# Three pairs turned on TensorE instead of by DMA, ch2 weights in column halves, and another order of the output units

## The chip, the cores and the metric

The kernel runs on one core of one Trainium2 chip. The time is device time in microseconds (us) of one execution. The kernel before takes 389.54 us (median of 3 runs, 389.31 to 390.26); the profiled execution has a span of 388.6 us from the first to the last instruction.

## The reference

Cosine attention is followed by an MLP mixer. There are 8 batches, 12 heads, 448 positions and a head size of 64.

```python
q_n = q / (np.linalg.norm(q, axis=-1, keepdims=True) + 1e-06)
k_n = k / (np.linalg.norm(k, axis=-1, keepdims=True) + 1e-06)
scores = np.matmul(q_n, k_n.transpose(0, 1, 3, 2)) / tau
scores = scores - np.max(scores, axis=-1, keepdims=True)
attn = np.exp(scores)
attn = attn / (np.sum(attn, axis=-1, keepdims=True) + 1e-09)
x = np.matmul(attn, v)                       # then heads side by side: [8, 448, 768]
h = np.maximum(x^T @ w_tok1, 0.0) @ w_tok2   # over positions: 448 -> 256 -> 448
u = x + h^T
h2 = np.maximum(u @ w_ch1, 0.0) @ w_ch2      # over channels: 768 -> 1536 -> 768
out = u + h2
```

All inputs and the output are float32.

## The kernel before

**Pairs.** The work runs over 48 pairs of heads (six pairs for each batch, `NPAIR`; `i` is the pair's number). For a pair, q and k are loaded by DMA, squared (GpSimd, or ScalarE early on), summed over the head (VectorE, `sums`), turned into reciprocal norms (`norms`: ScalarE, then VectorE) and scaled into a float16 tile `kq` (`scaled`, GpSimd). This tile has to be turned, so that the head's channels lie on the partitions; the turned tile is `qk`. `score` (L323) multiplies k against q into PSUM tiles `psS`, and ScalarE takes the exponential into `pt` (L324). Each pair has three such score tiles ahead of the first unit and a fourth after it: of the same kind up to pair 11, and from pair 12 on a smaller one (`score_rest`, tile `psQ`, L330) for the 64 rows that 3 x 128 leave over. `pv_rest` (L345) and `pv` (L362) multiply `pt` with v into two tiles `psO`, and VectorE divides (L365, L366) into `x`. `tok1` (tile `psR`, L393, result `rt`, L396) and `tok2` (tile `psU`, L407, result `u`, L410) are the mixer over positions. The result `u` is turned by DMA into `ut` (`udma`, L416), or for a few early pairs on TensorE.

**Turning kq.** Pairs below `DMA_T0` = 13 are turned on TensorE by `tpose`: eight transposes into a PSUM tile `pst` (L300) and a copy on VectorE into `qk` (L302). Pairs from 13 on are turned by a DMA transpose that SyncE issues (`tpose_dma`, L308). `side` also decides by `DMA_T0` where the load of the pair six ahead stands in SyncE's queue: ahead of everything for the earlier pairs, behind the DMA transpose for the later ones.

**Units.** The mixer over channels is cut into units that are put into a list (`refill`), batch by batch: twelve units of `m_ch1` (tile `psG`, six matmuls, L433, emptied by ScalarE at L436), then the units of `m_ch2` (tile `psF`, twelve matmuls, L449). A ch2 unit computes one column half (384 of 768) of one tile of 128 output rows; VectorE adds `u` to it into an output tile `ost` (L453), and after the second half SyncE writes it out (L468, L474). 448 rows are three tiles of 128 rows and 64 rows more; the 64 rows of two neighbouring batches share one tile, m = 3, which is computed with the odd batch. Its sum takes two VectorE instructions of 64 rows each, because the two halves come from two batches.

**Order of the work.** It is written out by hand. The main loop over pairs issues: the three score tiles; `pv_rest` and `pv` of the pair before; `side` (loads and the norms and scaling of later pairs); a first unit; `psQ`; `tok2` of pair i-2; `tpose` of the next pair if it is turned on TensorE; further units as long as the due matmul time (`fed`) asks for them; `tok1` of pair i-1. Below, a segment is what lies between two groups of score tiles. A segment thus has a first unit, right behind `pv`, and none to several last ones between `tok2` and `tok1`.

**PSUM.** Two pools share the banks. `ps` has two narrow buffers of one bank each (tag "b"), taken in turn by `pst`, `psO`, `psR`, `psU` and by units called without `wide`. `ps2` has three buffers of two banks each (tag "s"), taken in turn by `psS`, `psQ` and by units called with `wide`. A new tile waits until the tile before it in the same buffer has been read.

**Weights.** `weights_ch2` loads `moe_w_ch2` with two DMAs from GpSimd, which also convert to float16. Each takes half of the 1536 rows and all 768 columns; they are issued in `side` at pairs 8 and 10. Each ch2 unit needs all 1536 rows of its column half.

**The end.** After the last pair's scores there are a unit (`unit()`, narrow), the last `pv`, a few wide units, the last `tok1` and `tok2`, and then all units of the last batch.

Of the kernel before, what the change touches and what calls it, by code (L numbers as in the profile page):

```python
# [7 lines left out]
FP32 = mybir.dt.float32  # L8
# [14 lines left out]
def kernel(  # L23
# [12 lines left out]
    nc = tc.nc  # L36

    B, H, S, E = q.shape
    D = H * E
# [7 lines left out]
    DH = 384  # L47
# [3 lines left out]
    NHALF = 2 * B  # L51
    inv_tau = 1.0 / float(tau)
    EPS_NORM = 1e-6
    DMA_T0 = 13
    OLD = 2 * NPAIR


# [15 lines left out]
    def pieces(lo, hi):  # L73
        got = []
        while lo < hi:
            c = lo // SC
            end = min(hi, SC * (c + 1))
            got.append((c, lo - SC * c, end - SC * c))
            lo = end
        return got  # L80
# [6 lines left out]
    outp = ctx.enter_context(tc.tile_pool(name="outp", bufs=3))  # L87
# [33 lines left out]
    def load_qk(i):  # L121
        b, h0 = i // NPAIR, 2 * (i % NPAIR)
        n = i // HP
        half.setdefault(n, {})
        st = pipe[i] = {}
        st["q"] = qkv.tile([SC, QS, E], FP32, name=f"qf_{i}", tag="qf")
        nc.sync.dma_start(out=st["q"][:].rearrange("p (g c) e -> p g (c e)", g=2),
                          in_=q[b, h0:h0 + 2].rearrange("g (p c) e -> p g (c e)", c=NCH))
        st["k"] = load_rows(i, "k", k[b], 7)
        if not old(i) and "kr" not in half[n]:  # L130
            half[n]["kr"] = load_rest(i, "k", k[b])

    def load_v(i):
        pipe[i]["v"] = load_rows(i, "v", v[i // NPAIR], 4)
        if not old(i) and "vr" not in half[i // HP]:
            half[i // HP]["vr"] = load_rest(i, "v", v[i // NPAIR])
# [13 lines left out]
    wc2t = cst.tile([128, CT, D], FP16, name="wc2t")  # L150
# [40 lines left out]
                            in_=moe_w_ch1[128 * t:128 * t + 384, cols].rearrange("(t p) c -> p t c", p=128))  # L191

    def weights_ch2(i):
        nc.gpsimd.dma_start(out=wc2t[:, 6 * i:6 * i + 6, :],
                            in_=moe_w_ch2[768 * i:768 * (i + 1)].rearrange("(t p) d -> p t d", p=128))

# [11 lines left out]
    def cast_v(i):  # L210
        vt = vts[(i // HP) % NV]
        if old(i):
            nc.gpsimd.tensor_copy(out=vt[0:SC, i % HP, :, 0:E], in_=pipe[i]["v"][:])
            return
        nc.gpsimd.tensor_copy(out=vt[:, i % HP, 0:2 * KC, 0:E], in_=pipe[i]["v"][:])
        if i % HP == 0:
            nc.gpsimd.tensor_copy(out=vt[:, :, 2 * KC, 0:E], in_=half[i // HP]["vr"][:])
# [21 lines left out]
    def squares(i):  # L239
        square(i, 0)  # L240
        square(i, 1)
# [13 lines left out]
    def norms(i, a0=0, a1=2, dve=False):  # L255
        st = pipe[i]
        n, sl = some(i, a0, a1)
        rn = st["rn"][0:n, sl]
        ne = nes[i % 3][0:n, sl]
        if dve:  # L260
            nc.vector.tensor_reduce(out=rn, in_=ne, axis=AXX.X, op=ALU.add)
            nc.vector.reciprocal(out=rn, in_=rn)  # L262
            return
        nc.scalar.activation(out=rn, in_=st["ssq"][0:n, sl], func=AF.Ln, bias=tiny[0:n])
        nc.scalar.activation(out=ne[:, :, 0], in_=rn, func=AF.Exp, scale=0.5)
# [21 lines left out]
    def scaled(i):  # L287
        scale(i, 0)
        scale(i, 1)
# [14 lines left out]
    def tpose_dma(i):  # L304
        st = pipe[i]
        qk = att.tile([128, 2 * NCH * 128], FP16, name=f"qk_{i}", tag="qk")
        st["qk"] = qk[:].rearrange("p (a c s) -> p a c s", a=2, c=NCH)
        nc.sync.dma_start_transpose(out=st["qk"].rearrange("p a c s -> p (a c) s"),  # L308
                                    in_=st["kq16"][:].rearrange("p a c g e -> p (a c g e)"))
# [88 lines left out]
    def tok2(i, pe=False, wide=False):  # L398
        st = pipe[i]
        b, pj = i // NPAIR, i % NPAIR  # L400
        if pj == 0:
            u16[b] = mix.tile([128, DT, 4, 128], FP16, name=f"u16_{b}", tag="u16", bufs=4)
            ut[b] = mix.tile([128, DT, 4, 128], FP16, name=f"ut_{b}", tag="ut")
        psU = (ps2 if wide else ps).tile([128, 4, 128], FP32, name=f"psU_{i}", tag="s" if wide else "b")
        for m, lo in enumerate(windows(b)):
            for tt in range(TT):
                nc.tensor.matmul(psU[:, m], w2t[:, tt, lo:lo + 128], st["rt"][:, tt],  # L407
                                 start=(tt == 0), stop=(tt == TT - 1))
        u = u16[b][:, pj]
        nc.vector.tensor_tensor(out=u, in0=psU[:], in1=st["x"][:], op=ALU.add)  # L410
        if not pe:
            udma(i)
# [25 lines left out]
    ost = {}  # L438


    def m_ch2(b, m, lo, hi, st, wide):
        gt = gts[b // 2]
        at = 384 if m == 3 else 128 * m + (b % 2) * 512
        if lo == 0:
            ost[0] = outp.tile([128, D], FP32, name=f"ost_{b}_{m}", tag="ost")
        o = ost[0]
        psF = (ps2 if wide else ps).tile([128, 512], FP32, name=f"psF_{b}_{m}_{lo}", tag="s" if wide else "b")
        for ct in range(CT):
            nc.tensor.matmul(psF[:, 0:hi - lo], gt[:, ct, at:at + 128], wc2t[:, ct, lo:hi],  # L449
                             start=(ct == 0), stop=(ct == CT - 1))  # L450

        def add(p0, p1, bb, slot):
            nc.vector.tensor_tensor(out=o[p0:p1, lo:hi].rearrange("p (j e) -> p j e", e=128),  # L453
                                    in0=psF[p0:p1, 0:hi - lo].rearrange("p (j e) -> p j e", e=128),
                                    in1=u16[bb][p0:p1, lo // 128:hi // 128, slot], op=ALU.add)

        if m < 3:
            add(0, 128, b, m + b % 2)
        else:
            add(0, 64, b - 1, 3)  # L460
            add(64, 128, b, 0)
        if st is None:
            return
        if m < 3:
            r = 0
            for n, (c, p0, p1) in enumerate(pieces(*MAIN[m])):
                eng = nc.scalar if st and n == 0 else nc.sync
                eng.dma_start(out=out[b].rearrange("(p c) d -> c p d", c=NCH)[c, p0:p1, st:hi],  # L468
                              in_=o[r:r + p1 - p0, st:hi])
                r += p1 - p0  # L470
        else:
            (c, p0, p1), = pieces(384, S)
            for bb, r in ((b - 1, 0), (b, 64)):
                nc.sync.dma_start(out=out[bb].rearrange("(p c) d -> c p d", c=NCH)[c, p0:p1], in_=o[r:r + 64])  # L474

    def ns(cols, n=1):
        return n * (cols / 2.4 + 2.5)
# [4 lines left out]
    def ch2_units(b):  # L482
        cuts = ((0, DH, None), (DH, D, 0))
        ends = ((0, DH, None), (DH, D - 128, 0), (D - 128, D, D - 128))
        return [(ns(hi - lo, CT), lambda wide, m=m, lo=lo, hi=hi, st=st: m_ch2(b, m, lo, hi, st, wide))
                for m in ((3, 0, 1, 2) if b == B - 1 else range(3 + b % 2))
                for lo, hi, st in (ends if (b, m) == (B - 1, 2) else cuts)]

    queue = []
    fed = [0.0, 0.0]  # L490
# [1 line left out]
    def unit(wide=False):  # L492
        if queue:
            t, fn = queue.pop(0)
            fn(wide)
            fed[0] -= t
# [6 lines left out]
    def refill(b):  # L503
        new = ch1_units(b) + ch2_units(b)
        fed[1] = (sum(t for t, _ in new) - (KEPT if b == 0 else 0.0)) / (NPAIR + 1 if b == 0 else NPAIR)
        queue.extend(new)

    with tc.manual_schedule():
        for i in range(3):
# [9 lines left out]
            name=nc.get_next_instruction_name(), act_func_set_id=ACT_SET_LN_EXP,  # L519
# [77 lines left out]
        i = NPAIR  # L597
# [22 lines left out]
        def side(i):  # L620
            if i + 6 < NP_ALL and i + 2 < DMA_T0:
                load_qk(i + 6)
            cast_v(i)
            if i + 3 < NP_ALL:
                squares(i + 3)
            if i in (8, 10):
                weights_ch2((i - 8) // 2)
            if i + 2 < NP_ALL:
                norms(i + 2)
                norms(i + 2, dve=True)  # L630
                scaled(i + 2)
                if i + 2 >= DMA_T0:
                    tpose_dma(i + 2)
            if i + 6 < NP_ALL and i + 2 >= DMA_T0:
                load_qk(i + 6)
            if i + 4 < NP_ALL:
                load_v(i + 4)

        for i in range(NPAIR + 1, NP_ALL):
            b, pj = i // NPAIR, i % NPAIR  # L640
# [12 lines left out]
            elif pj == 2 and b > 1:  # L653
                refill(b - 1)
            side(i)
            fed[0] += fed[1]
            unit(True)
# [4 lines left out]
            if i > NPAIR + 1:  # L662
                tok2(i - 2)
            if i + 1 < DMA_T0:
                tpose(i + 1)
# [5 lines left out]
            if i + 3 < NP_ALL:  # L671
                sums(i + 3)
        last = NP_ALL - 1
        unit()
        pv_rest(last)
        pv(last, 0)
        pv(last, 1)
# [45 lines left out]
```

## Time and profile before

| What | Value |
|---|---|
| Time, median of 3 runs | 389.54 us |
| Span of the profiled execution | 388.6 us |
| TensorE busy with matmuls | 371.9 us (96%) |
| GpSimd, ScalarE, VectorE busy | 237.4, 226.5, 216.7 us |
| psG, psF matmuls (L433, L449) | 116.6 and 116.2 us |
| Score tiles psS (L323) | 41.9 us in 312 matmuls |
| Transposes pst (L300) | 7.9 us in 104 matmuls |
| Copies qk<-pst (L302), 128x1024 | 0.68 us for one |
| DMA transposes qk<-kq (L308) | 35, median 3.1 us from issue to landing |
| wc2t loads (L194) | 2 of 1152 KB (float16), 12.1 and 13.6 us to landing |

The profile gives each instruction's start and length per engine, the idle time before it and who ended that idle time. Ends of matmuls are modelled, and neighbouring matmuls overlap in it, so their lengths add up to more than the time they take. The distance between the starts of two groups is the safer measure. A wait is named by the instruction that came last before it ended. The chain of work is followed back from the last instruction of the kernel.

### The profile page before, as it was taken

How to read it: one execution, taken by the hardware profiler on the slowest of the kernel's cores; microseconds unless marked ns; L12 is line 12 of the kernel's file. 1: busy time of each engine (PE TensorE's matmuls, PEld its weight loads, DVE VectorE, ACT ScalarE, POOL GpSimd, SP SyncE). 2: the span in 40 equal slices, each digit the busy share in tenths (PEclk: the TensorE clock that was granted, in tenths of full speed). 3: DMA queues.
4: the chain of work that ended last, by engine and by line, in shares of the span. 5: the costliest groups of instructions: out<-in, count | busy, mean ns of one | idle time of the engine just before them, and what ended most of it. 6: DMA issues, size and time to landing. Idle time of an engine off the chain costs nothing.

```text
span 388.6 us, 10171 instructions
## 1 busy us (share of the span) xinstructions
PE 371.9 (96%) x4100; PEld 241.4 (62%) x4100; DVE 216.7 (56%) x517; ACT 226.5 (58%) x398; POOL 237.4 (61%) x383
## 2 busy tenths in 40 slices
PE   5889999979999999999999999999999999999995
PEld 5566666656657666667657666667656666565563
DVE  7799766766437574557536674557545673241031
ACT  5999687745666447846665447855665456501500
POOL 8899979877667587577567577678567642000000
PEclk9899999999999999999999999999999999999999
DMA  8999999999976977869896999859974854013022
GB/s 223 273 224 234 178 251 214 196 191 192 235 180 143 205 178 192 200 152 176 209 182 130 222 181 199 165 145 189 224 179 117 164 123 96 14 56 96 0 75 89
DMA packets 117055, 65.00 MB, mean 167 GB/s; under 512 B 74896, under 2 KB 113424, under 8 KB 117008
## 3 DMA queue, kind: packets, MB, share of 16 engines
q1 hardware_dynamic: 112112, 58.41, 68.8%
q0 software_dynamic: 4080, 5.21, 7.9%
q10 hardware_dynamic: 816, 0.73, 0.7%
q8 instruction: 32, 0.52, 0.6%
q14 instruction: 15, 0.12, 0.1%
HBM read 43.45 MB, written 11.01 MB: 140 GB/s over the span
## 4 chain that ended last, share of the span: by engine, by line
PE 84%; ACT 7%; DVE 3%; DMA 2%; POOL 1%; issue 1%; ACTq 0%; DVEq 0%; POOLq 0%
PE psG L433 28%; PE psF L449 27%; PE psO L362 9%; PE psS L323 7%; PE psU L407 5%; ACT pt L324 5%; PE psR L393 4%; PE psQ L330 2%; PE psO L345 1%; ACT sq L235 1%; DMA qk<-kq 1%; DVE ost L453 1%; DMA qf<-in_q_dram 1%; DVE ssq L253 1%; PE pst L300 1%
## 5 line engine op out<-in xcount | busy, mean ns | idle before, releaser
L324 ACT ACTIVATE pt<-psS 128x896 f16<-128x896 f32 (+1 forms) x156 | 132.5, 916 | 58.5 <-PE psS L323 58.5
L433 PE MATMUL psG<-ut,wc1t 128*128 128x448 f16 x576 | 116.6, 352 | 0.2 <-ACT gt L436 0.2
L449 PE MATMUL psF<-wc2t,gt 128*128 128x384 f16 (+2 forms) x684 | 116.2, 323 | 0.0
L276 POOL TENSOR_TENSOR kq<-kf,rn 128x384 f16<-128x384 f32 (+1 forms) x48 | 42.8, 892 | 76.7 <-DVE rn L262 72.5
L436 ACT ACTIVATE gt<-psG 128x448 f16<-128x448 f32 x96 | 51.8, 540 | 63.4 <-PE psG L433 63.4
L449 PEld LDWEIGHTS <-gt 128*128 128x128 f16 x684 | 64.3, 98 | 38.0
L433 PEld LDWEIGHTS <-wc1t 128*128 128x128 f16 x576 | 53.9, 98 | 44.5 <-issue 0.3
L453 DVE TENSOR_TENSOR ost<-psF,u 128x384 f32<-128x384 f32 (+2 forms) x65 | 34.7, 534 | 60.6 <-PE psF L449 59.1
L253 DVE TENSOR_REDUCE ssq<-sq 128x15 f32<-128x960 f32 (+2 forms) x49 | 55.8, 1141 | 4.1 <-ACT sq L235 2.3
L396 DVE TENSOR_SCALAR rt<-psR 128x256 f16<-128x256 f32 x48 | 20.2, 420 | 59.5 <-PE psR L393 59.4
L276 POOL TENSOR_TENSOR kq<-qf,rn 112x512 f16<-112x512 f32 x45 | 46.9, 1043 | 3.0
L323 PE MATMUL psS<-qk 64*128 64x448 f16 x312 | 41.9, 357 | 6.4 <-DVE qk L302 2.5
L362 PE MATMUL psO<-vt,pt 128*128 128x65 f16 (+1 forms) x1056 | 40.3, 193 | 0.2 <-DVE ut L424 0.2
L237 POOL TENSOR_TENSOR sq<-qf 112x512 f32<-112x512 f32 x39 | 40.5, 1039 | 0.0
L237 POOL TENSOR_TENSOR sq<-kf 128x384 f32<-128x384 f32 (+1 forms) x46 | 40.1, 872 | 0.0
L362 PEld LDWEIGHTS <-pt 128*128 128x128 f16 (+1 forms) x1056 | 35.2, 97 | 4.0 <-PE psS L323 1.0
L366 DVE TENSOR_TENSOR x<-psO,rec 128x256 f16<-128x256 f32 x84 | 35.7, 425 | 2.9
L410 DVE TENSOR_TENSOR u<-psU,x 128x512 f16<-128x512 f32 x48 | 32.4, 674 | 4.8 <-PE psU L407 3.6
L393 PEld LDWEIGHTS <-w1t 128*128 128x128 f16 x384 | 24.9, 98 | 8.6 <-issue 1.9
L407 PEld LDWEIGHTS <-w2t 128*128 128x128 f16 x384 | 24.9, 98 | 7.8 <-issue 1.5
L407 PE MATMUL psU<-rt,w2t 128*128 128x128 f16 x384 | 29.3, 219 | 0.2 <-DVE qk L302 0.2
L393 PE MATMUL psR<-x,w1t 128*128 128x128 f16 x384 | 29.3, 219 | 0.0
(54 smaller groups left out, 277.3 us busy)
## 6 DMA issues: line engine op xcount, KB each, us to landing
qf<-in_q_dram SPq DMA_DIRECT2D x48, 224.0 KB, 3.6
kf<-in_k_dram SPq DMA_DIRECT2D x36, 192.0 KB, 3.5
vf<-in_v_dram SPq DMA_DIRECT2D x36, 192.0 KB, 3.9
vf<-in_v_dram SPq DMA_DIRECT2D x12, 224.0 KB, 7.2
out_dram<-ost SPq DMA_DIRECT2D x8, 336.0 KB, 3.3
wc1t<-in_moe_w_ch_dram POOLq DMA_DIRECT2D x4, 576.0 KB, 9.8
wc2t<-in_moe_w_ch_dram POOLq DMA_DIRECT2D x2, 1152.0 KB, 12.8
out_dram<-ost SPq DMA_DIRECT2D x8, 288.0 KB, 3.3
```

Source lines behind the costliest of these rows:

```text
L237: nc.gpsimd.tensor_mul(out=dst, in0=src, in1=src)
L253: nc.vector.tensor_reduce(out=st["ssq"][0:n, sl], in_=st["sq"][0:n, sl], axis=AXX.X, op=ALU.add)
L276: eng.tensor_tensor(out=kq[0:p, a, 0:n].rearrange("p c g e -> p g c e"), in0=st["kq"[a]][:].rearrange("p (g c) e -> p g c e", g=2), in1=_b ...
L323: nc.tensor.matmul(psS[:, hh, 0:S], qk[hb, c * n:c * n + 128], qm[hb], start=True, stop=True)
L324: nc.scalar.activation(out=pts[i % 2][0:n, 2 * S * c:2 * S * (c + 1)].rearrange("p (h s) -> p h s", h=2), in_=psS[0:n, :, 0:S], func=AF.Ex ...
L362: nc.tensor.matmul(psO[:, m, 0:E + 1], pts[i % 2][0:n, at:at + 128], vt[0:n, i % HP, nch * hh + c, 0:E + 1], start=(old(i) and c == 0), st ...
L393: nc.tensor.matmul(psR[:, tt], w1t[:, w1[m], tt * 128:(tt + 1) * 128], st["x"][:, m], start=(m == 0), stop=(m == 3))
L407: nc.tensor.matmul(psU[:, m], w2t[:, tt, lo:lo + 128], st["rt"][:, tt], start=(tt == 0), stop=(tt == TT - 1))
L433: nc.tensor.matmul(psG[:, 0:S], wc1t[:, dt, ct * 128:(ct + 1) * 128], ut[b][:, dt].rearrange("p m s -> p (m s)")[:, lo:lo + S], start=(dt ...
L436: nc.scalar.activation(out=gt[:, ct, (b % 2) * S:(b % 2 + 1) * S], in_=psG[:, 0:S], func=AF.Relu)
L449: nc.tensor.matmul(psF[:, 0:hi - lo], gt[:, ct, at:at + 128], wc2t[:, ct, lo:hi], start=(ct == 0), stop=(ct == CT - 1))
L453: nc.vector.tensor_tensor(out=o[p0:p1, lo:hi].rearrange("p (j e) -> p j e", e=128), in0=psF[p0:p1, 0:hi - lo].rearrange("p (j e) -> p j e" ...
```

## The change

Four things are changed, each with what it needs.

- Pairs 13, 14 and 15 are turned on TensorE like the pairs before them (`DMA_T0` = 16). The first pair whose scores wait for a DMA transpose is then pair 16. The loads in `side` move with it.
- The ch2 weights come in two column halves in place of row halves, the second one pair later (pair 11). Batch 0's units take the left half of all three row tiles first and the right half after, so that the second load has more time. Three output tiles are then open at once, hence `ost[m]` in place of `ost[0]`.
- In the other even batches nothing changes. In the odd batches 1, 3 and 5 the left half of the rest row tile (m = 3) is moved one place ahead in the list, so that it is the first unit of its segment and not the last. The last batch keeps its order.
- The unit after the last pair's scores takes a wide PSUM buffer, so that the two narrow ones are left to `psO`.

```diff
-    DMA_T0 = 13
+    DMA_T0 = 16
...
     def weights_ch2(i):
-        nc.gpsimd.dma_start(out=wc2t[:, 6 * i:6 * i + 6, :],
-                            in_=moe_w_ch2[768 * i:768 * (i + 1)].rearrange("(t p) d -> p t d", p=128))
+        cols = slice(DH * i, DH * (i + 1))
+        nc.gpsimd.dma_start(out=wc2t[:, :, cols], in_=moe_w_ch2[:, cols].rearrange("(t p) d -> p t d", p=128))
...
-            ost[0] = outp.tile([128, D], FP32, name=f"ost_{b}_{m}", tag="ost")
-        o = ost[0]
+            ost[m] = outp.tile([128, D], FP32, name=f"ost_{b}_{m}", tag="ost")
+        o = ost[m]
...
+        if b == B - 1:
+            order = [(m, c) for m in (3, 0, 1, 2) for c in (ends if m == 2 else cuts)]
+        elif b == 0:
+            order = [(m, c) for c in cuts for m in range(3)]
+        else:
+            order = [(m, c) for m in range(3) for c in cuts]
+            if b % 2:
+                order[5:5] = [(3, cuts[0])]
+                order.append((3, cuts[1]))
         return [(ns(hi - lo, CT), lambda wide, m=m, lo=lo, hi=hi, st=st: m_ch2(b, m, lo, hi, st, wide))
-                for m in ((3, 0, 1, 2) if b == B - 1 else range(3 + b % 2))
-                for lo, hi, st in (ends if (b, m) == (B - 1, 2) else cuts)]
+                for m, (lo, hi, st) in order]
...
-            if i in (8, 10):
-                weights_ch2((i - 8) // 2)
+            if i in (8, 11):
+                weights_ch2((i - 8) // 3)
...
-        unit()
+        unit(True)
         pv_rest(last)
```

## The prediction

> **What bounds the kernel now.** I read the page's busy shares and slices first.
>
> ```profile
> span 388.6 us, 10171 instructions
> PE 371.9 (96%) x4100; PEld 241.4 (62%) x4100; DVE 216.7 (56%) x517; ACT 226.5 (58%) x398; POOL 237.4 (61%) x383
> PE   5889999979999999999999999999999999999995
> ```
>
> TensorE is busy in all but 16.7 us; no other engine passes 61%. So the end moves only if TensorE loses work or idle time. Busy time by stretches of 10 us puts 7.4 us of the idle time before 40 us and 4.4 in the last stretch, which the change leaves alone. The other 4.9 lie in a few places. The waits of TensorE name them, and its instructions in order of time show each. Ends of matmuls are modelled, so I measure by distances between starts, not by idle time.
>
> ```profile
> 78.77 0.61 PE L393 MATMUL psR<-x,w1t 128*128 128x128 f16 x8
> 79.94 0.74 PE L323 MATMUL psS<-qk 64*128 64x448 f16 x6 [0.56 <-DMA qk<-kq]
> ...
> 84.08 0.61 PE L393 MATMUL psR<-x,w1t 128*128 128x128 f16 x8
> 86.19 0.74 PE L323 MATMUL psS<-qk 64*128 64x448 f16 x6 [1.50 <-DMA qk<-kq]
> ...
> 92.28 0.61 PE L393 MATMUL psR<-x,w1t 128*128 128x128 f16 x8
> 93.41 0.74 PE L323 MATMUL psS<-qk 64*128 64x448 f16 x6 [0.52 <-DVE rt L396]
> ```
>
> These are the scores of pairs 13, 14, 15, the first three that a DMA turns. See the distance from psR to psS: 1.17, 2.11 and 1.13 us. (The third wait is booked to rt, but the weight load beside it to the DMA qk, which landed 3.5 us after its issue at 89.84.) An undisturbed segment and a disturbed one later on:
>
> ```profile
> 131.85 0.61 PE L393 MATMUL psR<-x,w1t 128*128 128x128 f16 x8
> 132.40 0.74 PE L323 MATMUL psS<-qk 64*128 64x448 f16 x6
> ...
> 133.21 0.92 PE L362 MATMUL psO<-vt,pt 128*128 128x65 f16 x24
> ...
> 138.50 0.61 PE L393 MATMUL psR<-x,w1t 128*128 128x128 f16 x8
> 139.04 0.55 PE L323 MATMUL psS<-qk 64*128 64x448 f16 x4
> 139.88 0.36 PE L323 MATMUL psS<-qk 64*128 64x448 f16 x2 [0.29 <-DVE ost L453]
> ...
> 140.55 0.93 PE L362 MATMUL psO<-vt,pt 128*128 128x65 f16 x24
> ```
>
> Undisturbed, psR to psS is 0.55 and psR to the long psO group 1.36. In the second it is 2.05: the third score tile waits for its PSUM buffer, which VectorE empties with the two half adds of a rest row tile (1.12 us from 138.70; rt only behind them). The same is at 227 and 315. Last, the end of the pairs:
>
> ```profile
> 336.92 0.61 PE L393 MATMUL psR<-x,w1t 128*128 128x128 f16 x8
> 337.71 1.29 PE L433 MATMUL psG<-ut,wc1t 128*128 128x448 f16 x6 [0.18 <-ACT gt L436]
> ...
> 339.64 0.28 PE L345 MATMUL psO<-vt,pt 64*128 64x65 f16 x7 [0.50 <-ACT gt L436]
> ```
>
> That unit takes one of the two narrow PSUM buffers; the second psO tile needs it and waits until ScalarE has emptied it at 339.58.
>
> **What the Trainium skill says.** "TensorE: Matmul & The Clock Gate", the step-by-step part: matmuls stay in program order, only weight loads are pulled ahead. The trace agrees: at 86.19 all stands behind one score tile. "Perfetto Trace Analysis", Optimizing Tensor Performance, Matmuls: groups should rotate through PSUM banks so that emptying one overlaps the next; the stalls at 139.88 and 339.64 are where the rotation is too short. "VectorE: DVE Perf Modes", The three transpose paths: a 128x128 tile takes 390 ns on TensorE and 1309 ns by DMA. In a stream the trace shows far less on TensorE: eight in the 0.45 us from 70.57 to 71.01 on the chain, 56 ns each. "DMA: Bandwidth & Descriptors", Specifications: pieces of 512 B or more move at line rate. The new halves read 1,536 B and write 768 B per row, so this speaks against a loss; no run yet shows these shapes.
>
> **The change, part by part.**
>
> *Transposes of pairs 13 to 15.* Added on TensorE: 3 x 0.45 = 1.35 us, and on VectorE three copies of 0.68 (the row 128x1024 from pst). Removed: waits of (1.17-0.55) + (2.11-0.55) + (1.13-0.55) = 2.76 us. New waits: in pairs 12 and 14 a second psF of 1.95 us follows the transposes, which hides the copy. In pair 13 no unit follows (the trace has psF once, at 81.50), only tok1. With psU starting at T: psU to T+0.45, transposes to T+0.90. VectorE starts u at T+0.65 (84.28 after 83.63) and hands on at T+1.26; the copy ends near T+1.95. tok1's psR takes the buffer that psU held, so it waits from T+0.90 to about T+1.35; the scores of 14 start at T+2.0. Before they started at T+2.56 (86.19-83.63): 0.56 gained. Behind the waiting psR stand the scores, and behind the copy rt, which the psO tiles need only later. Pair 13: 0.62-0.45 = 0.17; pair 15: 0.58-0.45 = 0.13. Sum **0.86 us**. Bounds: nothing of the wait in pair 13 (0.55 more), or as the early pairs, which have the same copy on their path: waits for qk L302 of 2.5 us in 5, the longest 0.7. With 0.7 in each of the three, 2.76-1.35-2.1 = -0.7.
>
> The inputs are there: GpSimd finishes kq of pair 13 at 73.65 and of 14 at 79.45, ahead of the transposes at 76.8 and about 84. Loads that now stand ahead in SyncE's queue concern pairs 17 to 19; the first DMA transpose left, pair 16, starts in a quieter queue than at 94.21 and is used at 101.5.
>
> *Rest row tiles first.* In batches 1, 3, 5 the units count off in the chain as one (118.88), two (121.47), three (125.53), four and five (128.12), six (134.13), seven (136.72), eight (141.47). The first rest half was seventh, the last of its segment; now it is sixth, with tok2 and a whole psF behind it. VectorE then does the two adds from 136.2 to 137.3 and u to 138.0; the seventh unit's single add ends at 139.26, before the third score tile at 139.42. Saved: 2.05-1.36 = 0.69, times three = **2.07 us**. Bounds: 0 if the wait moves to psU's buffer, 2.07 if nothing is left.
>
> *The last unit wide.* psG starts at 336.92+0.55 = 337.47, takes 1.14 (chain) and then psO 0.22: the long psO group at 338.83, not 339.85 (its row). All narrow buffers are free by 337.98 (rt at 337.56, 0.42 long). Saved **1.02 us**; all behind it is back-to-back TensorE work to the last psF, so it reaches the end.
>
> *Weights in column halves.* No matmul is added or taken. GpSimd issues two DMAs as before (0.88 each); the second, one pair later, falls into its idle 1.40 us ahead of 70.74. It leaves at about 69.4, not 62.7. Batch 0 needs the right half with its fourth unit, at 87.91 less the 0.73 gained by then, 87.1 or so. If bytes decide, it lands in 12.1 to 13.6 as before, by 83. If rows decide: 384 rows (wc1t) land in 9.8 and 768 in 12.8, so 1,536 in some 18.8 by the same slope, at 88.2: a wait of 1.1. If all of it scaled with rows, 25.6, at 95.0: a wait of 7.9. I take the bytes. The left half goes out at 50.3 as before and is used at 74.2; even 18.8 is early. Batch 0's three output tiles fill the three buffers, but the next output starts near 118.
>
> Sum: 0.86 + 2.07 + 1.02 = 3.95. Predicted 389.54 - 3.95 = **385.6 us**.
>
> **Rivals.**
> - *The right half comes late by its rows*: 385.6 + 1.1 = 386.7. For it: the slope of 3 us per 384 rows. Against: rows now are half as long. Chance 0.10.
> - *Waits move on*: the copies cost as in the early pairs (1.55 more), or half of the rest tiles' gain stays (1.0 more): 386.6 to 387.2. For it: VectorE gets copies while it is 58 to 69% busy (70 to 100 us); the add at 139.26 has only 0.16 to spare. Against: segments with one single add last show no wait (132.40). Chance 0.13.
> - *Slower than before*: the half takes 25.6 us, 385.6 + 7.9 = 393.5; or a transpose of ut meets the weights and batch 1's first psG (97.55) waits. Against the latter: its last transpose went out at 87.43 and landings take 3.6, so 6.5 us are to spare. Chance 0.04.
> - *More*: the pair 13 wait falls out too, 385.1. Chance 0.05.
>
> **How the numbers follow.** The forecast has the remaining 0.68 and sets the time. The range 384.8 to 387.1 takes in the first rival, nearly all of the second and the last; outside remain the slow case and what I have overlooked. Faster by over 0.3% means under 388.4: all but the slow case and 0.03 of things that partly cancel. Faster 0.93, same 0.03, slower 0.04.
>
> **What would show it.** After: pst 128 in number, 32 of them 128x128; qk by DMA 32 times; no wait of psS for a DMA near 80 to 94; one short wait of psR or psS on VectorE in pair 13. No wait of psS on ost near 139, 226, 314. No wait of psO on gt near 338. TensorE idle some 4 us less and about as busy as before (the 1.35 us come in, waits that the modelled ends count as busy go). The prediction fails if psF of batch 0 waits for wc2t near 87, or if psS after a rest tile still waits.

## The result, and the profile after

The changed kernel takes 386.75 us (median of 4 runs, 386.57 to 387.20) against 389.76 us before: a ratio of 0.9924 with a 95% interval of 0.9907 to 0.9941, or 3.0 us (2.3 to 3.6). The forecast was 385.6 us, within 384.8 to 387.1: the measured time lies in that range, and the saving is 0.9 us smaller than the 3.95 that was forecast. The ratios and intervals here and below come from the fast runs alone, so a ratio is not the quotient of two medians, and the two can differ by some tenths of a per cent.

The busy shares of the changed kernel's page:

```profile
span 385.4 us, 10226 instructions
PE 372.2 (97%) x4124; PEld 243.3 (63%) x4124; DVE 217.4 (56%) x520; ACT 226.6 (59%) x398; POOL 237.8 (62%) x383
PE   5989899999999999999999999999999999999995
```

TensorE's busy time is nearly unchanged, its idle time 3.5 us less. The scores of pairs 13, 14 and 15 in the changed kernel, on TensorE in order of time:

```profile
80.35 0.61 PE L393 MATMUL psR<-x,w1t 128*128 128x128 f16 x8
80.89 0.74 PE L323 MATMUL psS<-qk 64*128 64x448 f16 x6
...
84.60 0.61 PE L407 MATMUL psU<-rt,w2t 128*128 128x128 f16 x8
85.05 0.61 PE L300 MATMUL pst<-id,kq 128*128 128x128 f16 x8
85.99 0.61 PE L393 MATMUL psR<-x,w1t 128*128 128x128 f16 x8 [0.34 <-DVE u L410]
86.59 0.74 PE L323 MATMUL psS<-qk 64*128 64x448 f16 x6
...
93.13 0.61 PE L393 MATMUL psR<-x,w1t 128*128 128x128 f16 x8
93.67 0.74 PE L323 MATMUL psS<-qk 64*128 64x448 f16 x6
```

None of these score tiles waits for a DMA any more. The one wait here is psR's in pair 13's segment: the buffer that it takes still holds psU until VectorE has made `u` from it. It is 0.94 us from the transposes to psR, where 0.45 would be without a wait. From psU to the scores of pair 14 it is 1.99 us (86.59 less 84.60); the forecast worked out 2.0. The segment behind the first rest row tile, and then the end of the pairs with the wide unit:

```profile
138.78 0.61 PE L393 MATMUL psR<-x,w1t 128*128 128x128 f16 x8
139.32 0.74 PE L323 MATMUL psS<-qk 64*128 64x448 f16 x6
...
140.13 0.92 PE L362 MATMUL psO<-vt,pt 128*128 128x65 f16 x24
```

```profile
335.10 0.61 PE L393 MATMUL psR<-x,w1t 128*128 128x128 f16 x8
335.55 1.30 PE L433 MATMUL psG<-ut,wc1t 128*128 128x448 f16 x6
336.78 0.29 PE L345 MATMUL psO<-vt,pt 64*128 64x65 f16 x8
337.01 0.92 PE L362 MATMUL psO<-vt,pt 128*128 128x65 f16 x24
```

From psR to the long psO group it is 1.35 us where it was 2.05, and at the end 1.91 where it was 2.93: all three score tiles and the psO tiles start without a wait.

To see where the time went I cut each profile by the starts of psR, one for each pair, since these hardly depend on modelled ends. Four measures follow: the start of psR of pair 6; the pairs that the DMA waits touch, from psR of pair 10 to psR of pair 14 (72.0 to 101.0 in the first profile of before), called the middle stretch below; from there to the last psR, that of pair 47; and from that one to the end of the span. From psR of pair 6 to that of pair 10 it is 25.4 us in every profile.

| Profile | psR of pair 6 at | pair 10 to 14 | pair 14 to 47 | pair 47 to the end |
|---|---|---|---|---|
| before, first | 46.6 | 29.0 | 243.2 | 44.5 |
| before, second | 48.3 | 27.9 | 243.2 | 44.6 |
| changed, first | 47.8 | 28.1 | 240.1 | 44.1 |
| changed, second | 47.0 | 28.1 | 240.1 | 44.2 |

From pair 14 to 47 it is 3.1 us shorter, as worked out for the rest row tiles and the last unit (2.07 + 1.02). The missing 0.9 us lies in the middle stretch: the changed kernel has the length that was forecast (29.0 - 0.86 = 28.1), but 29.0 was not the usual length where DMAs turn these pairs, as the runs below show.

The last column is some 0.35 us shorter, which the forecast did not have. It is 44.1 to 44.2 in the four profiles with pairs 13 to 15 turned on TensorE and 44.4 to 44.6 in the ten others. In all of them the last matmul starts 39.84 us behind that psR, and the last store lands 3.3 to 3.4 us after that matmul's start. SyncE then has six more semaphores to go through in the first profile of before and one in the changed kernel, at 0.06 us each. Why they stand in another order is not shown.

### The profile page after: what moved, and what is told of

It reads as the page before. It is cut to its first block, busy times and chain, and to the rows that moved or that the text cites. A ratio compares the mean times of both kernels' runs of the same rounds, so it can differ in the third digit from the quotient of the medians.

```text
span 385.4 us, 10226 instructions
## 1 busy us (share of the span) xinstructions
PE 372.2 (97%) x4124; PEld 243.3 (63%) x4124; DVE 217.4 (56%) x520; ACT 226.6 (59%) x398; POOL 237.8 (62%) x383
## 4 chain that ended last, share of the span: by engine, by line
PE 87%; DMA 4%; ACT 4%; DVE 2%; POOL 1%; issue 1%; ACTq 0%; DVEq 0%; POOLq 0%
PE psF L449 28%; PE psG L433 28%; PE psO L362 9%; PE psS L323 7%; PE psU L407 5%; PE psR L393 5%; DMA ut<-u 3%; ACT pt L324 3%; PE psQ L330 2%; PE psO L345 1%; DMA qf<-in_q_dram 1%; PE pst L300 1%; ACT sq L235 1%; POOL sq L237 1%; DVE ssq L253 0%
## 5 line engine op out<-in xcount | busy, mean ns | idle before, releaser
L276 POOL TENSOR_TENSOR kq<-qf,rn 112x512 f16<-112x512 f32 x45 | 46.9, 1043 | 3.0
```

The source lines that it names most:

```text
L276: eng.tensor_tensor(out=kq[0:p, a, 0:n].rearrange("p c g e -> p g c e"), in0=st["kq"[a]][:].rearrange("p (g c) e -> p g c e", g=2), in1=_b ...
```

## The experiments

Times are medians, each against runs of the kernel before on the same chip (389.57 to 389.63 us); the 95% interval of the ratio stands in brackets. The first theory is the prediction's: each part gives what its place in the chain showed. In some of the expectations the psR that bounds the middle stretch is numbered one too high: where they say pairs 11 to 15, or give 29.0 for before, the stretch from psR of pair 10 to psR of pair 14 is meant.

**The parts alone.** First the order of the rest row tiles.

```diff
-                for m in ((3, 0, 1, 2) if b == B - 1 else range(3 + b % 2))
-                for lo, hi, st in (ends if (b, m) == (B - 1, 2) else cuts)]
...
+            order = [(m, c) for m in range(3) for c in cuts]
+            if b % 2:
+                order[5:5] = [(3, cuts[0])]
+                order.append((3, cuts[1]))
```

> Only the order in batches 1, 3 and 5 is changed: the left half of the rest row tile one place ahead. First theory (each part gives what its place in the chain showed): 2.07 us faster, 0.69 at each of three places, no wait of the third score tile on ost near 139, 227 and 315. Rival (the wait moves to another PSUM buffer): the time stays within 0.7 us of before and a wait on u or rt takes its place.

387.67 us, ratio 0.9955 [0.9940, 0.9969]: 1.2 to 2.3 us faster. No wait on ost is left, and pair 14 to 47 takes 241.1, 2.1 less. The first theory holds.

```diff
         last = NP_ALL - 1
-        unit()
+        unit(True)
```

> Only the unit after the last pair's scores is made wide. First theory: 1.02 us faster, psO of the last pair with no wait on gt, and psR to the long psO group 1.9 us in place of 2.9. Rival (the wide buffers are short there too): under 0.3 us faster, with a wait of a later wide unit on VectorE or ScalarE.

388.92 us, ratio 0.9978 [0.9957, 0.9999]. No wait on gt is left, and pair 14 to 47 takes 242.1, some 1.05 less. The first theory holds; its size rests on the profile, since the times allow anything from nothing to 1.7 us.

```diff
-    DMA_T0 = 13
+    DMA_T0 = 16
```

> Only pairs 13 to 15 are turned on TensorE; weights and orders as before. First theory: 0.86 us faster, with the three DMA waits gone and one wait in pair 13. Rival (the DMA waits in the profiled run of before were longer than in most runs, so that the 1.35 us of transposes buy little): between 0.3 us faster and 0.7 us slower in the median, though its profile shows no DMA wait in pairs 13 to 15.

390.83 us, ratio 1.0017 [0.9999, 1.0035]: no faster, by the ratio 0.7 us slower (0 to 1.4) and by the medians 1.2. Its profile shows no DMA wait in these pairs and a middle stretch of 28.1, the same as in the changed kernel. The first theory fails and the rival holds in direction: the 28.1 was right, and what it replaces is shorter than 29.0 in all other profiles in which DMAs turn pairs 13 to 15. The loss by the medians is larger than the 0.7 that the rival allowed.

```diff
-        nc.gpsimd.dma_start(out=wc2t[:, 6 * i:6 * i + 6, :], ...)
+        nc.gpsimd.dma_start(out=wc2t[:, :, cols], ...)
...
-            if i in (8, 10):
+            if i in (8, 11):
...
+        elif b == 0:
+            order = [(m, c) for c in cuts for m in range(3)]
```

> Only the ch2 weights come in column halves, at pairs 8 and 11, with batch 0's left halves first. First theory (nothing on the path): within 0.3 us of before, the DMA waits of pairs 13 to 15 as before, some 2.7 us. Rival (the second load at pair 10 is what delays the DMA transposes): at least 1 us faster, with the waits of pairs 13 and 14 under half of 2.1 us.

390.92 us, ratio 1.0038 [1.0020, 1.0057]: slower by 0.8 to 2.2 us. Neither theory holds. Its TensorE, around pairs 13, 14 and 15:

```profile
80.05 0.61 PE L393 MATMUL psR<-x,w1t 128*128 128x128 f16 x8
81.57 0.74 PE L323 MATMUL psS<-qk 64*128 64x448 f16 x6 [0.92 <-DMA qk<-kq]
...
85.71 0.61 PE L393 MATMUL psR<-x,w1t 128*128 128x128 f16 x8
86.83 0.74 PE L323 MATMUL psS<-qk 64*128 64x448 f16 x6 [0.51 <-DMA qk<-kq]
...
92.92 0.61 PE L393 MATMUL psR<-x,w1t 128*128 128x128 f16 x8
93.46 0.74 PE L323 MATMUL psS<-qk 64*128 64x448 f16 x6
```

Pairs 13 and 14 wait, 15 does not. With the row halves at pair 10 (the runs of the rest tiles and of the wide unit) pair 13 did not wait, pair 14 waited 0.57 and 0.26 us, and pair 15 1.16 and 1.15. The DMA transpose of pair 13 landed 6.6 us after its issue here, against 5.4 and 5.0 there. That its wait goes with the place of the second load is not shown by this alone: the first profile of before has the row halves at pair 10 and a wait at pair 13 all the same, with 6.2 us to landing.

Pair 15 has another candidate, SyncE's queue. First the kernel before (first profile), then this one:

```profile
88.75 0.98 SPq L468 DMA_DIRECT2D out_dram<-ost  x2
89.84 1.31 SPq L308 DMA_TRANSPOSE qk<-kq  x1
```

```profile
87.32 1.24 SPq L416 DMA_TRANSPOSE ut<-u  x1
88.67 1.23 SPq L308 DMA_TRANSPOSE qk<-kq  x1
```

In before, two stores of an output tile of batch 0 are issued right ahead of pair 15's transpose. They stand there in all six profiles with row halves in which a DMA turns this pair, and its scores start 0.3 to 1.2 us late in each. With column halves batch 0 does its left halves first, so it has no whole tile to store by then; in the three such profiles the stores are not there, the transpose lands 3.1 us after its issue, and pair 15 does not wait, whether the load stands at pair 11 or 9. No run changes this order alone, so the stores as the cause are read from the queue and not shown by a run.

**Two by two.** With the rest tiles' order and the wide unit in all four, the TensorE turns and the column halves each in or out.

> The changed kernel once more, beside three with parts left out. Theory of parts that belong together (column halves take the second weight load away from the DMA transposes' place, and TensorE turns just the pairs that it would then meet): 3.0 us faster than before, and at least 0.7 us faster than either kernel with one of the two left out. Theory of parts that add up (only the rest tiles and the wide unit bring anything): slower than the kernel with these two alone, by 1 to 2 us.

> The changed kernel with the weights in row halves at pairs 8 and 10 and batch 0's order as before. Parts that belong together: 1.9 us faster than before (2.6 from rest tiles and wide unit as measured, 0.7 given back as in the run with the TensorE turns alone). My first working: 3.9 us faster.

> The changed kernel with pairs 13 to 15 still turned by DMA. Parts that belong together: 1 to 2 us faster than before (2.6 less the 1.3 that column halves alone cost), with DMA waits in pairs 13 to 15. My first working: 3.1 us faster, waits of 2.76 us in these pairs.

> Only the rest tiles' order and the wide last unit. By the two single runs: 2.6 us faster than before; by the chain: 3.1. If the theory of parts that add up holds, this is the fastest of the four.

| Rest order and wide unit, with | Median | Ratio |
|---|---|---|
| column halves and TensorE turns (the changed kernel) | 386.46 | 0.9920 [0.9898, 0.9943] |
| TensorE turns only | 387.61 | 0.9948 [0.9931, 0.9965] |
| column halves only | 387.13 | 0.9948 [0.9925, 0.9971] |
| neither | 386.28 | 0.9917 [0.9891, 0.9943] |

By the medians each of the two alone loses 0.9 to 1.3 us against neither, and both together 0.2, nothing that can be measured. That the TensorE turns lose without the column halves is clear by the times: the lowest of 22 times, 386.90, is hardly under the highest of the changed kernel's six, 387.07. For the column halves alone it is not: their times scatter from 385.9 to 392.0, eight of 22 are under 386.5, and the intervals overlap. So of the theory of parts that belong together one half holds and the other stays open, and together they bring nothing over neither of them. The kernel with neither one keeps the whole 3.3 us.

**The kernel before once more, and the load at another place.**

> The kernel before, unchanged, with a profile of its own. Theory of the odd profile (the first profile of before had longer DMA waits in pairs 13 to 15 than most runs): from psR of pair 11 to psR of pair 15 between 27.0 and 28.5 us, not 29.0, and psR of pair 6 later than 46.6, about 47 to 48. Rival (29.0 is usual for before): 28.7 to 29.3. The ratio to before should hold 1.

389.67 us, ratio 0.9989 [0.9964, 1.0015]. The middle stretch is 27.9, psR of pair 6 at 48.3: the first profile of before had a good start and a bad middle. The profiled run itself took 391.05 us. It also shows a wait that the first did not:

```profile
75.87 1.14 PE L449 MATMUL psF<-wc2t,gt 128*128 128x384 f16 x6
78.13 1.14 PE L449 MATMUL psF<-wc2t,gt 128*128 128x384 f16 x6 [1.12 <-DMA wc2t<-in_moe_w_ch_dram]
...
81.69 0.61 PE L393 MATMUL psR<-x,w1t 128*128 128x128 f16 x8
82.23 0.74 PE L323 MATMUL psS<-qk 64*128 64x448 f16 x6
```

Batch 0's first psF runs through the six row blocks of the first half of the weights and waits 1.12 us for the second row half, which landed 13.8 us after its issue at 64.30; in the first profile 12.1 had been just enough. This is what the column halves are good for. Pairs 13 to 15, after that, wait only 0.2 us in this profile: most of what its 27.9 has above the floor is the wait for weights, not for a turned pair. (The floor is the middle stretch without waits or transposes, 29.0 less 2.76, or 26.2 us.)

Then the changed kernel with pair 13 alone turned on TensorE:

```diff
-    DMA_T0 = 16
+    DMA_T0 = 14
```

> The changed kernel, but with pair 13 alone turned on TensorE (DMA_T0 = 14). By the floor of 26.2 us without waits or transposes, pairs 11 to 15 take 26.2 + 0.45 for one set of transposes + 0.7 for pair 14's DMA wait as in the runs with column halves = 27.35, against 28.1 in the changed kernel: 0.7 us faster than it, near 385.9. Rival (the DMA wait follows the first pair turned by DMA): pair 14 waits 1 to 1.6, no gain over the changed kernel.

386.47 us, ratio 0.9910 [0.9880, 0.9940]: by the medians the same as the changed kernel, not 0.7 less, though the interval has room for 0.7. The profile decides for the rival:

```profile
79.59 0.61 PE L393 MATMUL psR<-x,w1t 128*128 128x128 f16 x8
80.13 0.74 PE L323 MATMUL psS<-qk 64*128 64x448 f16 x6
84.28 0.61 PE L393 MATMUL psR<-x,w1t 128*128 128x128 f16 x8
86.49 0.74 PE L323 MATMUL psS<-qk 64*128 64x448 f16 x6 [1.59 <-DMA qk<-kq]
```

Pair 13 no longer waits, and pair 14, now the first that a DMA turns, waits 1.59 us where I had taken 0.7 from the runs before.

And the changed kernel with no pair from 13 on turned on TensorE and the second weight load two pairs earlier:

```diff
-    DMA_T0 = 16
+    DMA_T0 = 13
...
-            if i in (8, 11):
+            if i in (8, 9):
```

> Rest tiles' order, wide last unit and column halves, all pairs from 13 on turned by DMA, and the second weight load at pair 9 in place of 11, so that it is over before the first DMA transpose. Theory (the load beside them is what delays the transposes): pair 13 waits under 0.3 us, where it waited 0.8 to 1.0 with the load at pair 11, and pairs 11 to 15 take 26.2 to 27.2 us; the median 0.5 to 1 us below the run with the load at pair 11. Rival (the first transposes wait for SyncE's queue or for GpSimd, wherever the load stands): pairs 13 to 15 wait 1.3 us or more in all.

385.96 us, ratio 0.9896 [0.9858, 0.9933]. The theory of the load beside the transposes holds for pairs 13 and 14:

```profile
79.15 0.61 PE L393 MATMUL psR<-x,w1t 128*128 128x128 f16 x8
79.69 0.74 PE L323 MATMUL psS<-qk 64*128 64x448 f16 x6
83.84 0.61 PE L393 MATMUL psR<-x,w1t 128*128 128x128 f16 x8
84.39 0.74 PE L323 MATMUL psS<-qk 64*128 64x448 f16 x6
90.63 0.61 PE L393 MATMUL psR<-x,w1t 128*128 128x128 f16 x8
91.17 0.74 PE L323 MATMUL psS<-qk 64*128 64x448 f16 x6
```

All three pairs start 0.54 to 0.55 us behind psR, though a DMA turns them; the middle stretch is 26.4, within 0.2 us of the floor. With the load at pair 11 (the run with column halves only) TensorE stood at nearly the same place, psR ahead of pair 13 at 79.35 and here at 79.15, and pairs 13 and 14 lost 0.8 and 0.7 us. Their transposes landed 6.4 and 5.4 us after issue there, 5.1 and 3.9 here. For pair 15 this run decides nothing, since it waited at neither place. Each side is one profile; in the medians the difference is 1.2 us (387.13 to 385.96, on two chips), and the intervals of the two ratios just overlap. This is the lowest median and the lowest single time (385.04) of all, but its interval overlaps with that of the changed kernel, so it beats before clearly and the changed kernel only by its median.

> Rest tiles' order and wide last unit alone, a second time, on the same chip as the three others: 3.1 us faster than before, as the chain says and as the first run of it measured (3.3); pairs 11 to 15 between 27.0 and 28.5 us, varying from run to run.

386.26 us, ratio 0.9909 [0.9877, 0.9940], a middle stretch of 26.6 after 27.0 in its first profile. The times are as expected, and the stretch is even shorter than the 27.0 given. So the load at pair 10 can also go by with hardly a wait.

## Why the prediction was nearly right, point by point

- **What bounds it**: right for what the change was to gain, since both gains are idle time of TensorE. But 0.3 us behind the last matmul, and losses that no wait of TensorE shows (below), also move the time.
- **Rest row tiles first, 2.07 us**: right. 2.1 in the profile, 1.2 to 2.3 in the times, and no wait moved to psU or rt. In the changed kernel the two half adds run from 136.48 to 137.54 and `u` after them, out of the way.
- **Last unit wide, 1.02 us**: right. 1.02 between psR and the long psO group in the changed kernel (1.91 for 2.93), some 1.05 in the run with it alone.
- **The new work of the transposes** (1.35 us and some 0.55 in pair 13): right. The stretch is 28.1 us in all four profiles with pairs 13 to 15 turned on TensorE.
- **The waits that they remove, 2.76 us**: wrong, and it is the missing 0.9. The term was read from one profile. In eight profiles in which DMAs turn these pairs the stretch was 29.0, 28.1, 27.9, 27.8, 27.7, 27.7, 27.0 and 26.6, and 26.4 with the load at pair 9; against 28.1 the turns gain 0.9 in the worst and lose 1.7 in the best. With the first eight the mean is 27.7, so by the stretch alone the turns cost some 0.4 us. The range of the forecast reached to a loss of 0.7 for this part, but for another reason, the copies' waits.
- **What the stretch leaves out**: where DMAs turn these pairs, a late start goes with a short stretch on the whole. With psR of pair 6 at 46.6, 46.9 and 47.0 the stretch was 29.0, 28.1 and 27.7; with it at 48.5, in two profiles, 27.0 and 26.6. (The 27.9 at 48.3 has 1.1 us of waiting for weights in it.) The sum of both is 75.3 us on average in the eight profiles and 75.4 in the four with the TensorE turns. So the turns cost between nothing and 0.4 us. A reading that fits is that a transpose lands when its own queue lets it, so that TensorE waits less if it comes later; no run changed the start alone to show it.
- **Column halves, nothing on the path**: right for the changed kernel. The halves landed 15.0 and 13.1 us after their issue, the second at 83.5 (70.4 + 13.1), and psF took the right half at 88.15 without a wait. So neither rows alone (18.8) nor all of it by rows (25.6) decided. Wrong as a general statement: with these pairs turned by DMA, the load at pair 11 stands where the transposes of pairs 13 and 14 run, and these land later than with the load at pair 9. I took the weights as a question of when they are needed, and left out whom they hold up.
- **The sum**: 3.95 forecast, 3.0 measured (2.3 to 3.6). The rest tiles and the last unit give 3.1. The turns take up to 0.4 of it, and the shorter closing part, which was not forecast, gives some 0.35 back; that these two nearly cancel is luck.

Still open is why column halves alone cost as much as 1.5 us. Their profile shows 1.4 us of waits in pairs 13 and 14, but the profiles in which DMAs turn these pairs have as much on the average (27.7 less 26.2). Each series of times has one profile, and no run put the column halves at pair 10, so the shape of the load and its place are not separated. Open too is why the TensorE turns with row halves are 1.1 us slower than the changed kernel: their profile has the same stretches, and only 0.3 us outside the span differ (below).

## What to carry to other kernels

Here a wait for a compute engine in the steady part repeated to a hundredth of a microsecond (0.29 us at three places in each of five profiles, gone in all nine with the new order), so the forecast from one profile was good. The waits for DMAs in a crowded stretch came to anything from none to 2.8 us in the same stretch: look at a second profile of the same kernel before their full length is booked as a gain, and at where TensorE stands when the stretch begins. And before work is moved to the busiest engine to escape a DMA wait, look for the transfer or the queue entry that makes the DMA late; moving one load by two pairs removed the waits of pairs 13 and 14 in its profile without work for TensorE.

## What the runs showed of the hardware

- The start differs from run to run with nothing changed in it: psR of pair 6 stood at 46.6 and 48.3 us in two profiles of the kernel before, and between 46.8 and 48.5 in all others. Part of it is a wait of psG for the DMA transpose of `ut` (none to 1.2 us).
- Two kernels, those with the TensorE turns but row halves, took 2.1 us more than their span from first to last instruction; all others, the changed kernel too, some 1.8. So 0.3 us of their loss lies outside the traced work, as much as their shorter closing part had gained. Why is open.
- Twice as many pieces of half the length took at most little more time, though the places of the loads differ too. The row halves of the weights landed in 11.1 to 13.8 us in eight profiles; the column halves in 9.8 to 15.0 in the five with the second at pair 11, and in 14.7 and 17.9 with it at pair 9, where the two loads overlap. Their issue cost GpSimd 1.08 us in place of 0.88.
